# Second batch's attention in a fused attention and mixture-of-experts kernel: its place among the first group's matmuls

## The chip, the cores and the metric

The kernel runs on one core of one Trainium2 chip. The metric is the device time of one execution in microseconds (us), of which the median of several runs counts.

## What is computed

Three stages follow each other. In the reference, cut to what matters:

```
scores = q @ k.T / sqrt(64)             # 4 batches, 8 heads, 576 tokens, head width 64
scores += -2**-(h+1) * (i - j)          # kept where 0 <= i - j < 128, else -1e9
x = softmax(scores) @ v                 # as 2304 tokens x 512

g   = x @ w_gate                        # 512 -> 1536
x   = (g * sigmoid(g) * (x @ w_val)) @ w_out

# then 8 experts, the two best of each token by noisy logits:
out = sum over 2 of  weight * (relu(x @ w1[e]) @ w2[e])
```

## The kernel before

**Groups.** The 2304 tokens go through the gated layer in four groups of 512, 640, 512 and 640 tokens (`GRP`), one for each batch of attention. A group that begins before its batch takes 64 tokens of the batch ahead (`hold`). Attention of batch 0 runs first, alone. After that the work of group b and the attention of batch b+1 are interleaved.

**Precision.** A float32 number is held as a rounded high part and a low part (float32r, two slots of one tile), and a product is three matmuls (`three`, L295 to L297). Splitting takes a copy on ScalarE (ACT in the profile) and a subtraction on VectorE (DVE) or GpSimd (POOL).

**Weights.** During group 0 each of 36 weight blocks of 128x512 is read from memory in an unusual layout (`cs`), rebuilt by one pass on ACT (L227), one on POOL (L228) and two on DVE (L229, L230), written to a scratch tensor for later groups, and split by ACT (L270) and by POOL or DVE in turn (L271). `Convert.one` and `Stream.split` do this.

**A group** (`mlp1`) has two lists of quanta. `hidden` makes the 12 blocks of the hidden layer, two weight blocks each; in group 0 a quantum is half a weight block, six matmuls of 512 columns, so there are 48. Its results go through `sg`: tanh on ACT (L571), two passes on DVE that each read a PSUM bank (L572, L576), a copy on ACT that makes the high part `hT` (L577) and the subtraction that makes the low part (L578). `rows` is the second matmul, 24 quanta of six matmuls too, which read `hT`. So group 0 has 72 quanta.

**Attention** of a batch after the first (`attention`) is four pairs of heads, each a chain of 12 steps: transposes of q and k (L352, L356), evacuated by ACT (L361, L363); the scores of nine 64-row units in two sets, of five and four (`qk4`, L430), on the same two PSUM banks; for each set bias and minimum on DVE (L394), exp on ACT (L397), reciprocal on DVE (L398, L399) and normalization on POOL (L403); five transposes of the result (`pt`, L447), evacuated by ACT (L450, L452, L454, L463); and two products with v (`pv`, L477), whose result is copied by ACT (L493, the high part) and subtracted by DVE (L494, the low part) into `xT`, the input of the next group. Chunk c of the contraction of group b+1 reads what pair c wrote, so the last quarter of each of its accumulations needs the last pair.

**Order.** `merge(a, b, lead)` deals the steps of attention out over the quanta. That is the order in which the code is written. The instructions' order on each engine is made from it by the framework's scheduler, which moves ahead what it takes to be ready; on the chip each engine runs its own list in order. SyncE (SP) issues the loads and the stores of the scratch tensor in order too.

Of the kernel before, what the change touches and what calls it, by code (L numbers as in the profile page):

```python
# [22 lines left out]
def f32(ap):  # L23
    return ap.bitcast(F32)
# [3 lines left out]
def tile_alibi_window_attention__swiglu__noisy_top2_moe(  # L28
# [15 lines left out]
    nc = tc.nc  # L44
    B, H, S, D = q.shape
# [8 lines left out]
    HP = H // 2  # L54
# [22 lines left out]
    def bank(i):  # L77
        return psum.tile([128, 512], F32, name=f"b{i}", tag=f"b{i}")
# [36 lines left out]
    def load_nat(t, src, b, p, rest=None):  # L115

        eng = nc.scalar if src is k and (b, p) == (0, 0) else nc.sync
        for i in range(2):
            eng.dma_start(t[:, 0:4, i, :], src[b, 2 * p + i, 0:512, :].rearrange("(i p) d -> p i d", p=128))
        eng.dma_start(t[0:64, 4] if rest is None else rest, src[b, 2 * p:2 * p + 2, 512:576, :].rearrange("h p d -> p h d"))  # L120
        return t
# [46 lines left out]
    def buffers(b, p):  # L168
        return SET[p % 2 if b == 0 else 0]

    def load_qk(b, p):
        qn, kn = (buffers(b, p).nat(x) for x in ("qn", "kn"))
        NAT[b, p, "q"] = load_nat(qn, q, b, p)
        NAT[b, p, "k"] = load_nat(kn, k, b, p, qn[64:128, 4])

    def load_v(b, p):
        bf = buffers(b, p)
        NAT[b, p, "i"] = bf.nv % 2
        bf.nv += 1
        load_nat(bf.v[NAT[b, p, "i"]], v, b, p)  # L180
# [20 lines left out]
    class Convert:  # L201
# [7 lines left out]
        def load(self):  # L209
            m = self.n["l"]  # L210
            if m == UB:
                return
            self.n["l"] += 1
            t = cvp.tile([128, KC, 256], I32, name="cs", bufs=5)
            nc.sync.dma_start(t, dsrc[m])
            self.raw[m] = t.rearrange("p k (f w) -> p (k f) w", w=2)
# [76 lines left out]
    def three(ps, st, mv, first, last):  # L293

        nc.tensor.matmul(ps, st(0), mv(0), start=first, stop=False, skip_group_check=True)  # L295
        nc.tensor.matmul(ps, st(0), mv(1), start=False, stop=False, skip_group_check=True)  # L296
        nc.tensor.matmul(ps, st(1), mv(0), start=False, stop=last, skip_group_check=True)  # L297
# [4 lines left out]
    def new_xt(i, dt=F32R):  # L302
        return main.tile([128, 2, KC * GW], dt, name=f"xT{i % 2}")
# [4 lines left out]
    def xt_part(b, s):  # L308
        return XT[b][:, s, :].rearrange("p (c s) -> p c s", c=KC)

    def blocks(b):
        return GRP[b][1] // 128
# [21 lines left out]
    def attention(b, bk):  # L334
# [3 lines left out]
        def pair_items(p):  # L338
# [37 lines left out]
            def vp():  # L376
                st["v"], st["pt"] = bf.v[NAT[b, p, "i"]], bf.pt
                nxt(load_v)
# [118 lines left out]
            def nxt(load):  # L497
                n = p + (2 if b == 0 else 1)
                if n < HP:
                    load(b, n)  # L500
                elif b + 1 < B and n == HP:
                    load(b + 1, 0)

            def first():
# [8 lines left out]
                if (b, p) == (0, 1):  # L513
                    bias(p)

            rest = lambda: (tr("t")(), nxt(load_qk))
            v0 = lambda: (vp(), pt(0)())
            if b == 0:
# [17 lines left out]
    def gbank(b):  # L536
        gcount[0] += 1
        l = (0, 1, 2) if b < B - 1 else (0, 1, 2, 4, 5)
        return bank(l[gcount[0] % len(l)])

    def mlp1(b):

        base = b * UB
        n = GRP[b][1]
        cut = (0, n) if n <= 512 else (0, n // 2, n)

        def hh(s, f, sl):
            t, f = (HT[0], f) if f < NFA else (HT[1], f - NFA)
            return t[:, s, f * GW + sl.start:f * GW + sl.stop]

        def gv(f):
            st = {}

            def go(which, half, cs):
                def run():
                    u = base + 2 * f + which
                    sl = slice(cut[half], cut[half + 1])
                    w_ = sl.stop - sl.start
                    if cs.start == 0:
                        if half == 0:  # L560
                            ws.split(u + 3)
                        st["ps", which, half] = gbank(b)
                    w, ps = ws.tile[u], st["ps", which, half]
                    for c in range(cs.start, cs.stop):
                        three(ps[:, :w_], lambda s: w[:, s, c * 128:(c + 1) * 128],
                              lambda s: xt_part(b, s)[:, c, sl], c == 0, c == KC - 1)
                    if cs.stop < KC:
                        return
                    if which == 0:
                        t = wpool[1].tile([128, HW], F32, name="sg", bufs=3)[:, :w_]  # L570
                        nc.scalar.activation(t, ps[:, :w_], AF.Tanh, scale=0.5)  # L571
                        nc.vector.scalar_tensor_tensor(t, t, 1.0, ps[:, :w_], op0=OP.add, op1=OP.mult)  # L572
                        st["t", half] = t
                    else:
                        t = st["t", half]
                        nc.vector.scalar_tensor_tensor(t, t, 0.5, ps[:, :w_], op0=OP.mult, op1=OP.mult)  # L576
                        nc.scalar.activation(hh(0, f, sl), t, AF.Copy)  # L577
                        nc.vector.tensor_sub(hh(1, f, sl), t, f32(hh(0, f, sl)))  # L578
                return run
            parts = [slice(0, KC)] if len(cut) > 2 else [slice(0, 2), slice(2, KC)]  # L580
            return [go(w, h, cs) for w in range(2) for h in range(len(cut) - 1) for cs in parts]

        hidden = []
        for f in range(NF):
            hidden += gv(f)

        def yo(f, half):
            def run():
                u = base + 2 * NF + f
                if half == 0:  # L590
                    ws.split(u + 3)
                w = ws.tile[u]
                if f == 0 and half == 0:
                    std.l = dict(std.yo[blocks(b)])
                    YB1[b] = [bank(i) for i in range(blocks(b))]
                for i in range(2) if half == 0 else range(2, blocks(b)):
                    ps = YB1[b][i]
                    three(ps, lambda s: hh(s, f, slice(i * 128, (i + 1) * 128)), lambda s: w[:, s, :], f == 0, f == NF - 1)
                    if f == NF - 1:
                        if i == 0:  # L600
                            X2[b] = new_xt(b, F32)
                        o = X2[b][:, 0, i * DM:(i + 1) * DM]
                        if i % 2:
                            nc.vector.tensor_copy(o, ps)
                        else:
                            nc.scalar.activation(o, ps, AF.Copy)
                        r0 = GRP[b][0] + i * 128
                        nc.gpsimd.dma_start(x2d[r0:r0 + 128, 0:DM], o)
                if f == NF - 1 and half:
                    std.l = dict(std.gv)  # L610
            return run

        return hidden, [yo(f, h) for f in range(NF) for h in range(2)]
# [329 lines left out]
        scat[e, j] = s  # L943


    def merge(a, b, lead=0):
        n = 0
        for i, f in enumerate(a):
            f()
            while n < len(b) and (n + 1) * (len(a) - lead) <= (i + 1) * len(b):  # L950
                b[n]()
                n += 1
        for g in b[n:]:
            g()
# [22 lines left out]
    for b in range(B - 1):  # L977
        side = (post(b - 1, std) if b else []) + attention(b + 1, std)
        if b == 1:
            side.insert(len(side) // 2, zero_out)  # L980
        hidden, rows = mlp1(b)
        if b == 1:
            merge(hidden, side)
            merge(rows, [])
        else:
            merge(hidden + rows, side, 4)
        if b == 0:
            cv_cm.__exit__(None, None, None)
    b = B - 1
# [6 lines left out]
    side = post(b - 1, std) + route(0, T3, rt, True)  # L996
# [5 lines left out]
    n = len(side)  # L1002
# [3 lines left out]
    hidden, rows = mlp1(b)  # L1006
# [56 lines left out]
    with tc.If(n_over > 0):  # L1063
        with tc.tile_pool(name="ov", bufs=1) as ov:
            for e in range(E):
# [5 lines left out]
                with tc.For_i(CAP, n_e) as j:  # L1071
# [10 lines left out]
                    t = bank(0)  # L1082
# [49 lines left out]
```

## Time and profile before

| | |
|---|---|
| median of 3 runs | 1105.17 us (1104.94 to 1105.54) |
| profiled execution | 1102.93 us, its span 1101.1 us |
| TensorE (PE) busy | 1061.1 us, 96% |
| DVE, ACT, POOL busy | 525.6 us (48%), 477.7 us (43%), 444.6 us (40%) |
| mean granted TensorE clock | 0.995 |

PE's list begins with attention of batch 0; group 0's matmuls follow, mixed with attention of batch 1; from 191.93 us on they are those of group 1. A share of the whole span says little here, since the stages differ: in the first 150 us DVE is busier than anywhere else. Times below are us from the span's start; "busy" of PE is modelled, and the idle time before an instruction is what counts.

### The profile page before, as it was taken

How to read it: one execution, taken by the hardware profiler on the slowest of the kernel's cores; microseconds unless marked ns; L12 is line 12 of the kernel's file. 1: busy time of each engine (PE TensorE's matmuls, PEld its weight loads, DVE VectorE, ACT ScalarE, POOL GpSimd, SP SyncE). 2: the span in 40 equal slices, each digit the busy share in tenths (PEclk: the TensorE clock that was granted, in tenths of full speed). 3: DMA queues.
4: the chain of work that ended last, by engine and by line, in shares of the span. 5: the costliest groups of instructions: out<-in, count | busy, mean ns of one | idle time of the engine just before them, and what ended most of it. 6: DMA issues, size and time to landing. Idle time of an engine off the chain costs nothing. (4 is left out here: it accounts for less than half of the span.)

```text
span 1101.1 us, 18525 instructions
## 1 busy us (share of the span) xinstructions
PE 1061.1 (96%) x6694; PEld 905.7 (82%) x6694; DVE 525.6 (48%) x1258; ACT 477.7 (43%) x1229; POOL 444.6 (40%) x540
## 2 busy tenths in 40 slices
PE   6899999999999999999999999999999999999996
PEld 4566777989988777688997887988889898989894
DVE  7879973355410444124675345535353534343321
ACT  6666664466632466444543324424242323232210
POOL 5655654344434454443388323314141414141301
PEclk9999999999999999999999999999999999999998
DMA  8999754433323234331333506626263636353201
GB/s 205 260 290 300 249 178 117 123 91 85 88 73 117 82 101 105 87 109 58 87 90 115 179 5 198 196 87 201 87 188 93 184 93 187 103 168 111 71 28 42
DMA packets 158901, 143.93 MB, mean 131 GB/s; under 512 B 68238, under 2 KB 122542, under 8 KB 158800
## 3 DMA queue, kind: packets, MB, share of 16 engines
q1 hardware_dynamic: 147152, 108.89, 34.5%
q0 software_dynamic: 10448, 33.47, 9.4%
q8 instruction: 55, 0.90, 0.3%
q10 hardware_dynamic: 1200, 0.30, 0.1%
q14 instruction: 46, 0.38, 0.1%
HBM read 113.84 MB, written 28.91 MB: 130 GB/s over the span
## 5 line engine op out<-in xcount | busy, mean ns | idle before, releaser
L271 POOL TENSOR_TENSOR wu<-wst,wu 128x512 fp32r<-128x512 f32 x126 | 166.5, 1325 | 191.5 <-ACT wu L270 187.1
L270 ACT ACTIVATE wu<-wst 128x512 fp32r<-128x512 f32 x272 | 169.9, 629 | 137.1 <-PE b L297 63.0
L895 PE MATMUL b<-xT,wu 128*128 128x304 f32 (+2 forms) x1536 | 222.4, 303 | 1.2 <-ACT xT L882 0.6
L895 PEld LDWEIGHTS b<-xT,wu 128*128 128x128 f32 x1536 | 216.8, 188 | 5.0 <-DVE xT L883 1.9
L295 PE MATMUL b<-xT,wu 128*128 128x320 f32 (+1 forms) x576 | 200.4, 352 | 3.2 <-DVE sg L572 2.1
L296 PE MATMUL b<-xT,wu 128*128 128x320 f32 (+1 forms) x576 | 197.4, 343 | 0.8 <-DVE xT L494 0.6
L297 PE MATMUL b<-xT,wu 128*128 128x320 f32 (+1 forms) x576 | 197.0, 342 | 0.0
L295 PE MATMUL b<-wu,hTa 128*128 128x512 f32 (+1 forms) x482 | 192.8, 401 | 1.0 <-DVE sg L576 1.0
L296 PE MATMUL b<-wu,hTa 128*128 128x512 f32 (+1 forms) x482 | 188.9, 392 | 0.0
L297 PE MATMUL b<-wu,hTa 128*128 128x512 f32 (+1 forms) x482 | 187.5, 393 | 0.0
L271 DVE TENSOR_TENSOR wu<-wst,wu 128x512 fp32r<-128x512 f32 x146 | 105.8, 729 | 47.1 <-ACT wu L270 44.7
L295 PEld LDWEIGHTS b<-xT,wu 128*128 128x128 f32 x576 | 108.2, 189 | 17.8 <-issue 4.0
L296 PEld LDWEIGHTS b<-xT,wu 128*128 128x128 f32 x576 | 108.8, 189 | 10.1 <-issue 1.7
L297 PEld LDWEIGHTS b<-xT,wu 128*128 128x128 f32 x576 | 108.6, 189 | 9.0 <-issue 1.6
L902 DVE SCALAR_TENSOR_TENSOR hTa<-b,hTa 128x304 fp32r<-128x304 f32 (+2 forms) x128 | 57.2, 471 | 118.0 <-ACT hTa L901 117.9
L872 POOL DMA_INDIRECT xo<-x2d,gib x37 | 36.8, 994 | 183.4 <-PE b L879 165.5
L901 ACT ACTIVATE hTa<-b 128x304 fp32r<-128x304 f32 (+2 forms) x128 | 50.2, 423 | 139.3 <-PE b L895 139.1
L295 PEld LDWEIGHTS b<-wu,hTa 128*128 128x128 f32 (+1 forms) x482 | 88.9, 185 | 21.3 <-issue 1.8
L297 PEld LDWEIGHTS b<-wu,hTa 128*128 128x128 f32 (+1 forms) x482 | 88.7, 184 | 20.6 <-issue 0.2
L296 PEld LDWEIGHTS b<-wu,hTa 128*128 128x128 f32 (+1 forms) x482 | 89.1, 185 | 18.4 <-issue 0.2
L403 POOL TENSOR_SCALAR sx<-sx,sm 128x192 f32<-128x192 f32 (+2 forms) x126 | 60.2, 494 | 65.3 <-DVE sm L399 45.3
L882 ACT ACTIVATE xT<-b 128x512 fp32r<-128x512 f32 (+1 forms) x40 | 22.7, 572 | 136.4 <-PE b L879 136.4
(196 smaller groups left out, 1314.6 us busy)
## 6 DMA issues: line engine op xcount, KB each, us to landing
wst<-in_moe_w_dram SPq DMA_DIRECT2D x128, 256.0 KB, 3.2
wst<-wscr SPq DMA_DIRECT2D x108, 256.0 KB, 2.7
wscr<-wst SPq DMA_DIRECT2D x36, 256.0 KB, 3.6
cs<-in_moe_w_gate_dram SPq DMA_DIRECT2D x12, 512.0 KB, 6.2
cs<-in_moe_w_val_dram SPq DMA_DIRECT2D x12, 512.0 KB, 5.6
cs<-in_moe_w_out_dram SPq DMA_DIRECT2D x12, 512.0 KB, 4.6
out_dram<-zero SPq DMA_DIRECT2D x1, 4608.0 KB, 20.2
x2d<-xT POOLq DMA_DIRECT2D x18, 256.0 KB, 4.0
```

The lines of the kernel that those rows point to most:

```text
L270: nc.scalar.activation(t[:, 0, :], s, AF.Copy)
L271: self.eng(n).tensor_sub(t[:, 1, :], s, f32(t[:, 0, :]))
L295: nc.tensor.matmul(ps, st(0), mv(0), start=first, stop=False, skip_group_check=True)
L296: nc.tensor.matmul(ps, st(0), mv(1), start=False, stop=False, skip_group_check=True)
L297: nc.tensor.matmul(ps, st(1), mv(0), start=False, stop=last, skip_group_check=True)
L403: nc.gpsimd.tensor_scalar(x, x, sm[:, i:i + 1], 1.0, op0=OP.mult, op1=OP.mult)
L872: nc.gpsimd.indirect_dma_start(out=x[0:r], out_offset=None, in_=x2d[0:GRP[-1][0], :] if (e, g) == (0, False) else x2d, in_offset=bass.Indi ...
L882: nc.scalar.activation(d[0], tv, AF.Copy)
L895: nc.tensor.matmul(ps[g][:, 0:hi - lo], w[:, a, c * 128:(c + 1) * 128], xgt(e, m, g)[:, c, 0:hi - lo], start=(c == 0 and a + m == 0), stop ...
L901: nc.scalar.activation(d, ps[g][:, 0:hi - lo], AF.Relu)
L902: nc.vector.scalar_tensor_tensor(h2[1][:, f, lo:hi], ps[g][:, 0:hi - lo], 0.0, f32(d), op0=OP.max, op1=OP.subtract)
```

## The change

Attention of batch 1 is dealt out over quanta 22 to 68 of group 0's 72, where it was dealt out over quanta 0 to 68. `merge` gets an argument `late` for this. The loads of its first pair are no longer asked for by attention of batch 0, but by an entry put in at place 12 of `hidden`. And in group 0 the subtraction that makes the low part of `hT` (L578) goes to POOL.

```diff
-                elif b + 1 < B and n == HP:
+                elif 0 < b < B - 1 and n == HP:
                     load(b + 1, 0)
...
-                        nc.vector.tensor_sub(hh(1, f, sl), t, f32(hh(0, f, sl)))
+                        (nc.vector if b else nc.gpsimd).tensor_sub(hh(1, f, sl), t, f32(hh(0, f, sl)))
...
-    def merge(a, b, lead=0):
+    def merge(a, b, lead=0, late=0):
...
-            while n < len(b) and (n + 1) * (len(a) - lead) <= (i + 1) * len(b):
+            while n < len(b) and (n + 1) * (len(a) - lead - late) <= (i + 1 - late) * len(b):
...
-            merge(hidden + rows, side, 4)
+            if b == 0:
+                hidden.insert(12, lambda: (load_qk(1, 0), load_v(1, 0)))
+            merge(hidden + rows, side, 4, 0 if b else 22)
```

What the scheduler makes of it differs from pair to pair. Counted in quanta of six matmuls on PE's list, the first score matmuls of the four pairs stand at quantum 4, 22, 40 and 60 before, and at quantum 4, 37, 54 and 76 after. Quantum 72 is the first of group 1. From quantum 82 on the lists of PE are the same.

The first place is PE around that seam. Before, the last pair's scores were done eleven quanta ahead; its transposes (`sx`) and the first product with v stand among the last matmuls of group 0 (`hTb`), and the row with `xT1` and 320 columns opens group 1:

```order
L447 MATMUL b6_2114<-ident_74,sx4_96 128x128
L447 MATMUL b6_2114<-ident_74,sx4_96 64x128
L477 MATMUL b7_2125<-pt_91,v1_90 64x128 x4
L297 MATMUL b2_1827<-wu_2158,hTb_735 128x512
L295 MATMUL b3_1828<-wu_2158,hTb_735 128x512
L296 MATMUL b3_1828<-wu_2158,hTb_735 128x512
L297 MATMUL b3_1828<-wu_2158,hTb_735 128x512
L295 MATMUL b0_2295<-xT1_801,wu_2214 128x320
```

After, the last pair's scores (L430) themselves stand in group 1, with three matmuls of group 1 between them and the transposes that need their softmax:

```order
L430 MATMUL b5_2059<-kT_1881,qT_97 64x192 x2
L295 MATMUL b2_2268<-xT1_1071,wu_2197 128x320
L296 MATMUL b2_2268<-xT1_1071,wu_2197 128x320
L297 MATMUL b2_2268<-xT1_1071,wu_2197 128x320
L447 MATMUL b6_2102<-ident_74,sx0_92 64x128
L447 MATMUL b6_2102<-ident_74,sx0_92 128x128
L447 MATMUL b6_2113<-ident_74,sx1_93 128x128 x3
L477 MATMUL b7_2142<-pt_91,v1_90 64x128 x2
L447 MATMUL b6_2131<-ident_74,sx4_96 128x128
L447 MATMUL b6_2131<-ident_74,sx4_96 64x128
L477 MATMUL b7_2142<-pt_91,v1_90 64x128 x4
L447 MATMUL b6_2162<-ident_74,sx2_94 128x128 x3
```

So a whole chain of a pair moved from among group 0's matmuls to behind the seam. The two rows that follow the last of these are the first matmuls that read the last pair's chunk.

The second place is DVE in the same pair: the end of the first set (its minimum `mn`, then the reciprocal of its sums `sm`) and the start of the second. Before:

```order
L394 ISA mn_1961 128x1
L398 TENSOR_SCALAR sm_1962<-sm_1962 128x5
L399 RECIPROCAL sm_1962<-sm_1962 128x5
L271 TENSOR_TENSOR wu_2158<-wst_2102,wu_2158 128x512
L494 TENSOR_TENSOR xT1_801<-b7_1995,xT1_801 128x320
L394 ISA sx2_94,mn_2041<-b4_2031,tab0_76 128x192
```

After, the first set's sums are `sm_2004`, the second set's `sm_2069` (its minimum `mn_2068`):

```order
L394 ISA mn_2068 128x1
L399 RECIPROCAL sm_2004<-sm_2004 128x5
L398 TENSOR_SCALAR sm_2069<-sm_2069 128x4
L399 RECIPROCAL sm_2069<-sm_2069 128x4
L494 TENSOR_TENSOR xT1_1071<-b7_2142,xT1_1071 128x256
```

The reciprocal of the first set moved behind the whole second set's L394, which in turn stands behind the L494 of the pair before.

The third place is POOL in the hidden part of group 0. After:

```order
L271 TENSOR_TENSOR wu_1333<-wst_1255,wu_1333 128x512
L578 TENSOR_TENSOR hTa_723<-sg_1181,hTa_723 128x512
L228 TENSOR_SCALAR cs_1135<-cs_1135 128x512
L228 TENSOR_SCALAR cs_1219<-cs_1219 128x512
L271 TENSOR_TENSOR wu_1444<-wst_1336,wu_1444 128x512
L578 TENSOR_TENSOR hTa_723<-sg_1281,hTa_723 128x512
```

Where L228 and L271 of the weights stood alone, one L578 stands between them for every two weight blocks, twelve in all.

## Rows read from the trace of the kernel before

**Rows 1.** Three stretches: length, busy us and instructions by engine, clock, DMA share, GB/s.

```profile
62.33:155.10 92.77, 84.86 (x509) 64.25 (x505) 83.77 (x170) 64.84 (x174) 58.03 (x67) 0.98 0.84 264
101.60:107.60 6.00, 3.85 (x24) 2.78 (x24) 5.96 (x19) 4.29 (x14) 2.06 (x2) 0.73 0.90 269
155.10:205.24 50.14, 50.01 (x323) 40.95 (x323) 18.23 (x46) 24.82 (x68) 19.86 (x25) 1.00 0.43 124
```

**Rows 2.** PE's waits from 62 to 205 us: total us, times, longest.

```profile
PE b L295 <- DVE sg L572: 2.1, 2, 1.7
PE b L295 <- DVE sg L576: 1.9, 2, 1.0
PE b L477 <- ACT pt L463: 0.8, 1, 0.8
```

**Rows 3.** PE in order of time around 104 us: start, us, instruction, idle before.

```profile
103.78 1.09 PE L430 MATMUL b<-kT,qT 64*64 64x192 f32 x16 [2.15 <-DVE mn L394]
...
105.40 0.63 PE L296 MATMUL b<-xT,wu 128*128 128x512 f32 x1
105.83 0.63 PE L297 MATMUL b<-xT,wu 128*128 128x512 f32 x1
```

**Rows 4.** Groups by line and form, 62 to 205 us: busy us, mean ns; idle before.

```profile
L271 POOL TENSOR_TENSOR wu<-wst,wu 128x512 fp32r<-128x512 f32 x20 | 27.9, 1393 | 23.9 <-ACT wu L270 22.5 <-DMA qn<-in_q_dram 1.3
L229 DVE SCALAR_TENSOR_TENSOR wst<-wst,cs 128x512 int32<-128x512 int32 x30 | 26.2, 877 | 11.1 <-POOL cs L228 11.1
L230 DVE SCALAR_TENSOR_TENSOR wst<-cs,wst 128x512 int32<-128x512 int32 x30 | 25.9, 870 | 0.1
...
L572 DVE SCALAR_TENSOR_TENSOR sg<-sg,b 128x512 f32<-128x512 f32 x12 | 8.1, 674 | 0.7 <-ACT sg L571 0.7
L578 DVE TENSOR_TENSOR hTa<-sg,hTa 128x512 fp32r<-128x512 f32 x9 | 7.2, 799 | 1.0 <-ACT hTa L577 0.9
...
L578 DVE TENSOR_TENSOR hTb<-sg,hTb 128x512 fp32r<-128x512 f32 x3 | 2.1, 690 | 0.7 <-ACT hTb L577 0.7
```

**Rows 5.** POOL and DVE side by side near 94 us, in order of time.

```profile
93.89 1.23 POOL L228 TENSOR_SCALAR cs<-cs 128x512 f32<-128x512 f32 x1 [1.04 <-issue]
94.52 1.13 DVE L229 SCALAR_TENSOR_TENSOR wst<-wst,cs 128x512 int32<-128x512 int32 x1
```

**Rows 6.** Batch 1's second pair, first set: scores, first DVE row, normalization on POOL.

```profile
95.30 0.88 PE L430 MATMUL b<-kT,qT 64*64 64x192 f32 x20
...
101.77 0.34 DVE L394 CUSTOM_DVE_ANT_0 sx<-b,tab 128x192 f32<-128x192 f32 x1
...
106.94 2.19 POOL L403 TENSOR_SCALAR sx<-sx,sm 128x192 f32<-128x192 f32 x5 [0.36 <-DVE sm L399]
```

**Rows 7.** The same of batch 1's last pair: scores, last DVE row, normalization.

```profile
171.25 0.88 PE L430 MATMUL b<-kT,qT 64*64 64x192 f32 x20
...
173.38 0.08 DVE L394 DVE_READ_ACCUMULATOR2_ANT mn<- 128x1 f32 x1
...
175.34 2.37 POOL L403 TENSOR_SCALAR sx<-sx,sm 128x192 f32<-128x192 f32 x5 [3.01 <-ACT wu L270]
```

**Rows 8.** ACT evacuating one set of transposes, in order of time.

```profile
171.36 0.39 ACT L454 ACTIVATE pt<-b 128x256 f32<-128x256 f32 x1 [0.38 <-PE b L447]
171.64 0.54 ACT L463 ACTIVATE pt<-b 64x128 f32<-64x128 f32 x2
```

**Rows 9.** PE at the start of group 1, in order of time.

```profile
191.93 0.31 PE L295 MATMUL b<-xT,wu 128*128 128x320 f32 x1
192.07 0.31 PE L296 MATMUL b<-xT,wu 128*128 128x320 f32 x1
...
197.52 0.49 PE L447 MATMUL b<-ident,sx 128*128 128x128 f32 x3
197.94 0.66 PE L477 MATMUL b<-pt,v 128*64 128x128 f32 x8
198.53 0.41 PE L295 MATMUL b<-xT,wu 128*128 128x320 f32 x1
...
205.24 0.42 PE L677 MATMUL b<-xT,wgn 128*32 128x128 f32 x6
```

## The prediction

> **What bounds the kernel now.** I read first the table of stretches, then PE's waits, then PE in order of time around the longest wait, and last the groups by line. PE is busy 96% of the span, so only stretches where it is not can give anything, and of these the change touches one: group 0, from 62 us on. There the stretches [rows 1] show 7.9 us of PE idle to 155 us (92.77 less 84.86) and 0.1 us after that (50.14 less 50.01). DVE is busy 83.8 of 92.8 us in the first part and 5.96 of 6.00 us around the longest wait, but only 18.2 of 50.1 us in the second [rows 1]. So PE waits for DVE, which is full early and has room late. The waits say the same: two for L572 and two for L576, which free the PSUM banks of the hidden layer, 4.0 us in all [rows 2], and 2.15 us before a set of scores, for the minimum of the set before it, which holds its banks [rows 3]. Behind that idle time the granted clock is low: 0.73 on average over 6.00 us [rows 1], which is 3.2 us at the level of 1.2 GHz, and the matmuls follow each other at 0.43 us there [rows 3]. Half of 3.2 us is lost, 1.6 us. All that PE loses in this part of the program is thus 8.0 + 1.6 = **9.6 us**, and no better place for attention can win more.
>
> **What the change moves, and what it can't move.** The matmuls, their number and their columns stay. Work that goes from one place on PE to another costs nothing by itself. From quantum 82 on PE's list is unchanged, so everything is decided before the row that now starts at 205.24 us [rows 9].
>
> **The gain in group 0.** The first pair stays where it was, at quantum 4. The two longest waits for L572 and L576, 1.7 and 1.0 us [rows 2], lie at 67 and 71 us, ahead of quantum 12, where PE's list is the same: 2.7 us stay. At most 9.6 - 2.7 = 6.9 us can go. What relieves DVE: twelve subtractions leave it, 7.2 + 2.1 = 9.3 us [rows 4], and three of four pairs come later. What loads it: without attention PE asks for the weights faster. For two weight blocks DVE needs two passes L229 and L230 each, 2 x (0.877 + 0.870) = 3.5 us, one L271 of some 0.7 us (as L572, the nearest row that POOL does not disturb), and L572 with L576, 1.35 us [rows 4]: 5.5 us. PE needs for them 24 matmuls of 512 columns at 0.23 us (half of the 0.43 at half clock [rows 3], and a little): 5.5 us. The two are level, so DVE stays close behind PE and doesn't get ahead. Before, the second pair's scores on PE were 6.5 us ahead of DVE's first row for them (95.30 to 101.77) [rows 6]. Of what stands ahead of that place now and did not before, DVE has 8 weight blocks (14.0 us), 3 L271 (2.1) and 7 of L572 and L576 (4.7), less 5 L578 (4.0) [rows 4]: 16.8 us, up to 19 with what POOL adds (below). PE has 88 matmuls and four products, 88 x 0.228 + 0.6 = 20.6 us. So DVE is still 3 to 5 us behind. The normalized rows of that set then come about 2 us after PE wants its transposes (0.8 us of matmuls stand between). I put new waits at 3.7 us in all: these 2, half a microsecond for the third pair, and 1.2 us of the small ones as in the row for L463 [rows 2]. Gain 6.9 - 3.7 = **3.2 us**. Bounds: 6.9 us if nothing new waits, and -2 us if the second pair waits as long as before, the clock falls again (2.15 + 1.6 us) and the new waits come on top.
>
> **The subtraction on GpSimd.** L271 is the same operation on the same shape there: 12 x 1.39 = 16.7 us [rows 4], against 58 of 92.8 us that POOL is busy [rows 1]. Its readers are the `rows` quanta from 48 on, so nobody waits for its result. Queued behind it on POOL are L228 and L271 of the weights; no wait of PE there is for a weight (the long ones are for `sg` and the scores [rows 2, 3]), so I cost that at nothing. If that cover is gone, each costs up to 1.4 us.
>
> A price of it is on DVE. A DVE pass with two operands in SBUF is slowed when POOL works: L229 takes 1.13 us beside an L228 [rows 5], and the means of L229 and L230 are 0.88 and 0.87 us, while L572, with one operand in PSUM, stays at 0.67 [rows 4]. That is 0.2 us x 60 = 12 us over POOL's 58 us or more, 0.2 us of DVE for each us of POOL: 16.7 us of subtractions give back 3 of the 9.3 us.
>
> The Trainium skill (SBUF — State Buffer, Who interferes with whom) says that a DVE instruction with two SBUF inputs contends with a GpSimd instruction that reads SBUF, and that the later one fully blocks until the first is done. It speaks against this edit: by it a DVE pass that meets a subtraction waits for what is left of 1.39 us, and if each meets one halfway DVE loses 12 x 0.7 = 8.4 us, nearly all of the 9.3. The rows agree in kind (0.67 against 0.88) and give the smaller price.
>
> **The loads.** The nine DMAs of the first pair stand on SP within a few places of where they stood, among the same weight loads. Nothing, and a few tenths either way.
>
> **The loss at the seam.** Now the last pair's chain stands behind group 0's last matmul, with few matmuls around it, and the last quarter of every accumulation of group 1 needs it. I add it up from the seam, with PE's list in hand. (1) To the scores: 24 matmuls of 320 columns at 0.145 us (191.93 to 192.07) 3.5 us, three groups of transposes at 0.42 (197.52 to 197.94) 1.3 us [rows 9]; they share one bank, and two of its evacuations, 0.9 us each [rows 8], are waited for: 6.6 us. (2) Scores and minimum, 171.25 to 173.46: 2.2 us [rows 7], 8.8. (3) The second set's L394 now stands behind the L494 of the pair before, and that behind an evacuation and a product: 1.3 us, then four units at the pace of (2), 1.8 us, and only then the first set's reciprocal: 11.9. (4) Normalization starts 0.4 us later and takes 2.4 us for five [rows 7]: 14.7. (5) Transposes and evacuation 1.3 us, then the next transposes, the product and its copy at about that again, 1.4 us: **17.4 us** from the seam to the first matmul of the last chunk. PE's own work in that time: 27 matmuls 3.9, 29 transposes at 0.14 us 4.1, 18 products at 0.59 for four [rows 9] 2.7, 18 score matmuls at 0.88 for ten [rows 7] 1.6: 12.3 us. So 5.1 us are lost, and I add 1 us for the second product, whose chain is mostly covered by 18 matmuls. Before, the same stretch loses 0.1 us [rows 1]. The idle times inside are of the length of the one in [rows 3], so the clock should fall here; much of it falls on idle time: 0.6 us of the 1.6. Loss **6.7 us**. Bounds: from scores to normalization I have 5.7 us; the quiet pair took 4.1 (171.25 to 175.34) [rows 7], and without the clock and half of the last 1 us that is 4 us in all; the pair in the full stretch took 11.6 (95.30 to 106.94) [rows 6], which makes 12.6 us. I stay near the quiet one, since DVE and ACT are only half busy there [rows 1].
>
> **Sum.** 6.7 - 3.2 = +3.5 us. The profiled execution took 1102.93 us and would take 1106.4. The median is 2.24 us above it, so I predict **1108.7 us**. Ends: 4 - 6.9 = -2.9 and 12.6 + 2 = +14.6 us.
>
> **Rivals.** *Faster:* DVE gets free in the hidden part, all 6.9 us return, and the seam goes at the quiet pair's pace, 4 us: -2.9 us, 1102.3. For it speaks that DVE's relief is largest just where PE waits; against it that DVE and PE need the same 5.5 us for two blocks. It decides from where DVE reaches the second pair's L394 no more than 2 us after its scores and the seam loses under 4.7 us. *No change:* the waits only move, 5 lost at the seam and 5 won: 1105.2. For it speaks that both sums are of one size. *Slower by more:* the GpSimd subtractions block DVE and hold up the weights' passes queued behind them, so that the gain is nothing: +6.7 us, 1111.9. For it speaks [rows 5], against it the mean of 0.2 us for each us of POOL. The rule cited above is this rival's, and would give this time if every subtraction met a pass. That the change doesn't do what it says is true in part, since the first pair stays; it is in the sum.
>
> **How the numbers follow.** Forecast 0.50, faster 0.15, no change 0.20, slower by more 0.15. A measurement of this kernel tells 0.2%, 2.2 us, from no change. The forecast's own spread leaves 0.07 of its 0.50 within that. So faster 0.15, same 0.27, slower 0.58. The range from 1103 to 1114.5 leaves out the last of the faster case and the upper end of the seam.
>
> **What would show it.** In the new profile: group 1's first matmul starts 8 to 11 us earlier than 191.93, since 6.5 us of the last pair's work stand behind it now; the row at 205.24 starts 2 to 6 us later; PE's waits there name L403, L463 or L493, some 5 to 8 us in all; the 2.15 us wait is gone or smaller; L578 shows twelve times on POOL at 1.3 to 1.5 us. The forecast is wrong if PE idles under 4 us between the seam and that row, or if the waits ahead of the seam fall under 3 us.

## The result, and the profile after

The changed kernel takes **1119.65 us** (median of 4 runs, 1118.53 to 1121.32) against 1105.36 us of the kernel before in the same comparison: ratio 1.0122, 95% interval 1.0095 to 1.0149. That is about 13.5 us slower. The forecast was slower, 1108.7 us, with a range that ended at 1114.5: the direction is right, the time lies outside.

The profiled execution took 1118.53 us, its span is 1116.7 us, 15.6 us more than before. PE's busy share is the same (96%) and its mean clock close (0.991), so again only stretches tell something. The first fence answers [rows 1]; columns as there. Its second row is group 0 from 62.33 us to group 1's first matmul (191.45 us), the third goes from there to the L677 row:

```profile
62.33:155.10 92.77, 80.14 (x422) 60.45 (x419) 82.81 (x137) 57.59 (x140) 67.79 (x69) 0.98 0.81 256
62.33:191.45 129.12, 116.49 (x640) 88.96 (x637) 97.69 (x174) 76.13 (x193) 87.07 (x91) 0.99 0.69 217
191.45:218.88 27.43, 23.44 (x194) 18.69 (x192) 7.64 (x31) 13.59 (x49) 6.07 (x13) 0.88 0.38 102
```

The reader is to see three things. PE idles 12.6 us ahead of the seam (129.12 less 116.49) where it idled 7.9 [rows 1]. DVE, which lost eleven of the twelve subtractions and one of three pairs of attention from the first of these stretches, is nearly as busy as before: 82.8 against 83.8 us. And behind the seam PE idles 4.0 us (27.43 less 23.44) and runs at a clock of 0.88, which is some 3 us more.

PE's waits from 62 to 230 us (total us, times, longest), beside [rows 2]:

```profile
PE b L295 <- DVE sg L572: 4.8, 4, 1.4
PE b L447 <- POOL sx L403: 4.8, 3, 2.2
PE b L447 <- ACT pt L463: 1.9, 3, 0.7
PE b L430 <- DVE mn L394: 1.5, 2, 1.3
PE b L295 <- DVE sg L576: 1.2, 1, 1.2
```

The wait for L572 grew from 2.1 to 4.8 us, and the wait for the normalized rows (L403) from 0.5 to 4.8. In the kernel before it was this:

```profile
PE b L447 <- POOL sx L403: 0.5, 1, 0.5
```

Behind the seam the last pair's chain looks so (PE and POOL in order of time: start, us, instruction, idle before), to be read beside [rows 9]:

```profile
191.45 0.39 PE L295 MATMUL b<-xT,wu 128*128 128x320 f32 x1
...
198.26 0.88 PE L430 MATMUL b<-kT,qT 64*64 64x192 f32 x20
...
203.57 3.45 POOL L403 TENSOR_SCALAR sx<-sx,sm 128x192 f32<-128x192 f32 x9 [9.49 <-ACT sx L397]
...
204.34 0.67 PE L447 MATMUL b<-ident,sx 128*64 128x128 f32 x2 [1.71 <-POOL sx L403]
...
205.57 0.52 PE L447 MATMUL b<-ident,sx 128*128 128x128 f32 x3 [0.57 <-ACT pt L463]
...
207.01 0.69 PE L447 MATMUL b<-ident,sx 128*128 128x128 f32 x2 [0.55 <-ACT pt L463]
...
209.23 0.90 PE L295 MATMUL b<-xT,wu 128*128 128x320 f32 x2
...
218.88 0.42 PE L677 MATMUL b<-xT,wgn 128*32 128x128 f32 x6
```

Last, the groups that answer [rows 4], from 62.33 to 205.24 us (busy us, mean ns, idle before):

```profile
L229 DVE SCALAR_TENSOR_TENSOR wst<-wst,cs 128x512 int32<-128x512 int32 x29 | 30.8, 1066 | 8.3 <-POOL cs L228 8.3
L230 DVE SCALAR_TENSOR_TENSOR wst<-cs,wst 128x512 int32<-128x512 int32 x30 | 28.9, 970 | 0.3
L271 DVE TENSOR_TENSOR wu<-wst,wu 128x512 fp32r<-128x512 f32 x16 | 14.9, 928 | 3.4 <-ACT wu L270 3.1
L578 POOL TENSOR_TENSOR hTa<-sg,hTa 128x512 fp32r<-128x512 f32 x9 | 13.3, 1480 | 5.2 <-ACT hTa L577 5.2
L572 DVE SCALAR_TENSOR_TENSOR sg<-sg,b 128x512 f32<-128x512 f32 x12 | 8.1, 676 | 1.8 <-ACT sg L571 1.8
```

L229 went from 877 to 1066 ns, L230 from 870 to 970; L572, with an operand in PSUM, stayed at 0.68 us.

**Where the 15.6 us are.** What the lower clock costs is added up here over slices of 2 us, in both kernels alike: busy time times the missing share of the clock. Ahead of the seam: 12.6 us idle and 1.7 by the clock, 14.3, against 7.9 + 1.7 = 9.6 before: 4.7 more. From the seam to the L677 row: 4.0 + 3.2 = 7.2 us against 0.1 [rows 1]: 7.1 more. The L677 row itself is 13.64 us later (218.88 less 205.24), so 1.8 us are neither idle time nor clock by these views. From 62.33 us to that row both kernels have the same 831 matmuls, so these 1.8 us must lie inside rows that count as busy: a matmul that nothing follows counts 0.3 to 0.4 us, where in a row the same one costs 0.15 [rows 9]. No run prices that by itself. Further on, one more fall of the clock, which the forecast had no term for, costs 1.4 us (15.90 us busy at 0.91) behind a wait of 1.92 us. The same wait was 1.61 us before, and the clock stayed. The second row is of the kernel before:

```profile
468.00:486.00 18.00, 15.90 (x85) 11.71 (x78) 2.75 (x14) 9.59 (x29) 11.70 (x16) 0.91 0.37 98
...
454.40:471.00 16.60, 14.77 (x86) 10.76 (x79) 2.76 (x14) 9.52 (x29) 11.80 (x16) 1.00 0.37 106
```

### The profile page after: what moved, and what is told of

Its sections match the earlier page's. It is cut to its first block, busy times and chain, and to the rows that moved or that the text cites. A ratio compares the mean times of both kernels' runs of the same rounds, so it can differ in the third digit from the quotient of the medians.

```text
span 1116.7 us, 18534 instructions
## 1 busy us (share of the span) xinstructions
PE 1067.3 (96%) x6694; PEld 909.0 (81%) x6694; DVE 528.7 (47%) x1246; ACT 478.8 (43%) x1229; POOL 457.3 (41%) x552
## 4 chain that ended last, share of the span: by engine, by line
PE 83%; DVE 6%; ACT 4%; DMA 3%; issue 2%; POOL 1%; ACTq 0%; SPq 0%; POOLq 0%; DVEq 0%
PE b L295 19%; PE b L297 18%; PE b L296 18%; PE b L895 18%; PE b L477 3%; PE b L447 2%; PE b L879 1%; PE b L430 1%; DVE wst L229 1%; ACT sx L397 1%; PE b L352 1%; DVE wst L230 1%; DMA xo<-x2d,gib 1%; DMA wst<-in_moe_w_dram 1%; PE b L664 1%
## 5 line engine op out<-in xcount | busy, mean ns | idle before, releaser
L271 POOL TENSOR_TENSOR wu<-wst,wu 128x512 fp32r<-128x512 f32 x126 | 165.2, 1314 | 188.6 <-ACT wu L270 186.9
L270 ACT ACTIVATE wu<-wst 128x512 fp32r<-128x512 f32 x272 | 169.9, 630 | 148.3 <-PE b L297 57.8
L271 DVE TENSOR_TENSOR wu<-wst,wu 128x512 fp32r<-128x512 f32 x146 | 108.9, 750 | 47.4 <-ACT wu L270 45.2
L403 POOL TENSOR_SCALAR sx<-sx,sm 128x192 f32<-128x192 f32 (+2 forms) x126 | 59.2, 486 | 77.1 <-DVE sm L399 30.4
```

The source lines that it names most:

```text
L270: nc.scalar.activation(t[:, 0, :], s, AF.Copy)
L271: self.eng(n).tensor_sub(t[:, 1, :], s, f32(t[:, 0, :]))
L403: nc.gpsimd.tensor_scalar(x, x, sm[:, i:i + 1], 1.0, op0=OP.mult, op1=OP.mult)
```

## Experiments: the engine of the subtraction

Ratios below are to the kernel before, measured on the same chip, with 95% intervals. All kernels are ordered anew by the scheduler, so the places of the scores shift by some quanta from run to run; where that matters it is said.

**The changed kernel with L578 back on VectorE.**

```diff
-                        (nc.vector if b else nc.gpsimd).tensor_sub(hh(1, f, sl), t, f32(hh(0, f, sl)))
+                        nc.vector.tensor_sub(hh(1, f, sl), t, f32(hh(0, f, sl)))
```

> The changed kernel with group 0's L578 back on VectorE; the late placing and the early loads stay. Theory A (the subtraction on GpSimd slows VectorE's two-operand passes by as much as it takes off VectorE: L229, L230 and L271 there took 11.2 us more in the changed kernel, L578 took 9.3 us less): VectorE has about 2 us less to do before group 1, POOL 17 us less, group 1's first matmul comes 2 to 4 us earlier, time 1115 to 1118. Theory B (only the place of attention counts, not the engine of L578): 1118.5 to 1121. Theory C (the forecast's own step: GpSimd takes 9.3 us off and costs 3): group 0 gets 4 to 6 us worse, 1123 to 1126.

Measured 1114.31 us, 1.0065 (1.0048 to 1.0081): 0.57% less than the changed kernel. To give VectorE the work back made the kernel faster, a little more than A expected; theories B and C fall. PE idles 8.7 us ahead of the seam instead of 12.6, although DVE's sum is no smaller: L229, L230, L271 and L578 take 77.1 us there, the first three 74.6 in the changed kernel.

**The kernel before with only L578 moved** (its line as in the changed kernel).

> The kernel before with only group 0's L578 moved to GpSimd; attention and loads as before. Theory A (lock as dear as the relief): VectorE's busy time up to 206 us within 3 us of before, time 1105 to 1108, no gain. Theory B: 1104.5 to 1106. Theory C (relief of 6 us net): the waits for L572, L576 and for the scores' minimum go, 1100 to 1103.

Measured 1111.43 us, 1.0034 (1.0017 to 1.0050): slower than A's range, against C. PE idles 12.7 us in group 0 instead of 7.9. DVE's passes show why (62.33 to 205.24 us):

```profile
L229 DVE SCALAR_TENSOR_TENSOR wst<-wst,cs 128x512 int32<-128x512 int32 x30 | 33.1, 1112 | 11.3 <-POOL cs L228 11.3
L230 DVE SCALAR_TENSOR_TENSOR wst<-cs,wst 128x512 int32<-128x512 int32 x30 | 26.4, 889 | 0.3
L271 DVE TENSOR_TENSOR wu<-wst,wu 128x512 fp32r<-128x512 f32 x16 | 13.7, 857 | 4.0 <-ACT wu L270 4.0
```

Together 73.2 us. Before, the same three groups and L578 took 72.7 us in this stretch (25.5 + 25.9 + 12.0 + 9.3, with one L229 less). VectorE got nothing. The row of the kernel before that [rows 4] does not have is

```profile
L271 DVE TENSOR_TENSOR wu<-wst,wu 128x512 fp32r<-128x512 f32 x16 | 12.0, 747 | 3.3 <-ACT wu L270 3.0
```

**L578 on neither of the two**, in the changed kernel and in the kernel before:

```diff
-                        nc.vector.tensor_sub(hh(1, f, sl), t, f32(hh(0, f, sl)))
+                        if b:
+                            nc.vector.tensor_sub(hh(1, f, sl), t, f32(hh(0, f, sl)))
+                        else:
+                            nc.scalar.activation(hh(1, f, sl), t, AF.Copy, scale=0.0)
```

> The changed kernel with group 0's L578 replaced by a copy on ScalarE that writes zeros (the low part of the hidden layer is left out of the second matmul in group 0), so neither VectorE nor GpSimd has it. The order of the scores on PE is that of the changed kernel. Theory A (lock): L229 and L230 return to means of about 0.88 us, the waits for L572 and L576 before the second pair mostly go, time 1111 to 1115. Theory B (the place alone): 1118.5 to 1121. The part behind the seam should not change in either: 27 us from group 1's first matmul to the L677 row.

> The kernel before with group 0's L578 replaced by a copy on ScalarE that writes zeros (the low part of the hidden layer is left out of the second matmul in group 0). This is what the forecast took GpSimd's subtraction to be: VectorE's relief without its price. Theory A (VectorE's 9.3 us are worth something to PE when GpSimd does not take them): PE's idle time from 62 us to group 1 falls from 7.9 to 3 to 5 us, time 1099 to 1103. Theory B (VectorE's load there does not decide): 1104.5 to 1107.

Measured, in the changed kernel: 1108.06 us, 1.0014 (1.0001 to 1.0028), even less than A expected; in the kernel before: 1102.08 us, 0.9953 (0.9934 to 0.9972). So the work taken off VectorE is worth 0.5% if GpSimd doesn't get it. PE's idle time fell less than A had it in the kernel before, from 7.9 to 6.7 us and not to 3 to 5; the clock did not fall from 62 us to group 1. The two stretches of the changed kernel with this edit, ahead of the seam and behind it, and DVE's passes:

```profile
62.33:182.00 119.67, 114.91 (x655) 88.78 (x655) 89.95 (x175) 81.98 (x206) 66.91 (x79) 1.00 0.75 237
182.00:209.00 27.00, 23.31 (x197) 18.49 (x197) 7.73 (x31) 13.83 (x49) 6.18 (x13) 0.87 0.37 103
```

```profile
L229 DVE SCALAR_TENSOR_TENSOR wst<-wst,cs 128x512 int32<-128x512 int32 x30 | 28.3, 946 | 8.8 <-POOL cs L228 7.7 <-DMA wst<-wscr 0.5 <-DMA kn<-in_k_dram 0.5
L230 DVE SCALAR_TENSOR_TENSOR wst<-cs,wst 128x512 int32<-128x512 int32 x30 | 24.0, 800 | 0.5
L271 DVE TENSOR_TENSOR wu<-wst,wu 128x512 fp32r<-128x512 f32 x16 | 14.3, 894 | 1.5 <-ACT wu L270 1.4
```

PE idles 4.8 us ahead of the seam at full clock, and the stretch behind the seam is as in the changed kernel (3.7 us idle, clock 0.87). The three groups are 66.6 us against 74.6 in the changed kernel: twelve subtractions on GpSimd cost VectorE 8.0 us, if anything more, since the stretch of the changed kernel has one L229 less. In the order of the kernel before it is 73.2 less 64.8 (25.2 + 25.6 + 14.0), 8.4 us.

## Experiments: the seam and the place

**Ending eight quanta earlier**, with L578 on GpSimd, on ScalarE (zeros) and on VectorE:

```diff
-            merge(hidden + rows, side, 4, 0 if b else 22)
+            merge(hidden + rows, side, 4 if b else 12, 0 if b else 22)
```

> The changed kernel with attention dealt out over quanta 22 to 60 instead of 22 to 68; the last pair's scores then stand at quantum 65 and 67, no chain behind the seam. Theory S (the seam alone costs 6.8 us of idle time and half clock): that is gone, 2 us come back as waits among the rows of group 0, time 1112 to 1116. Theory D (what is taken from the seam is lost again in the denser part): 1118 to 1121. Group 0's hidden part should lose as much PE time as in the changed kernel, 12 us of idle time between 62 us and the last pair.

> The changed kernel with both suspects gone: attention dealt out over quanta 22 to 60, so that no chain stands behind the seam, and group 0's L578 replaced by the copy of zeros on ScalarE (its low part left out). If seam and GpSimd's subtraction are the two causes and add up (0.88% and 1.08% of the time by the runs so far, from 1.22% above before): 0.7% under before, 1097 to 1101. If the one hides the other: 1102 to 1106. Against the kernel before with the same copy on ScalarE it tells what the late place is worth by itself: the forecast had it worth some us, a rival nothing.

> The changed kernel with attention dealt out over quanta 22 to 60 and L578 on VectorE as before: only the late place and the early loads are left, with no chain behind the seam. If the parts add (0.57% for the subtraction, 0.88% for the seam): 0.2% under before, 1103 to 1106. If the late place costs by itself (three pairs in 30 quanta, VectorE full from 80 to 140 us): 1107 to 1111.

Measured: 1111.14 us, 1.0034 (1.0021 to 1.0046) with GpSimd; 1103.99 us, 0.9971 (0.9957 to 0.9985) with ScalarE; 1111.60 us, 1.0043 (1.0025 to 1.0062) with VectorE. In the first, the stretch from group 1's first matmul to the L677 row:

```profile
198.41:212.82 14.41, 14.17 (x116) 12.69 (x114) 3.55 (x8) 5.62 (x19) 3.38 (x5) 1.00 0.45 131
```

There the seam costs 0.24 us at full clock where it cost 7.2, and the whole is 0.88% less than the changed kernel: theory S, a little beyond it. Ahead of the seam PE idles 11.7 us, the 12 that were expected. The parts do not add, though. With seam and GpSimd's subtraction both gone, 0.7% under before was expected and 0.29% came; the kernel before with the same copy on ScalarE is at 0.9953, no worse. **The late place by itself is worth nothing** (together with its early loads, which no run parts from it). And with VectorE doing the subtraction, ending earlier brought 0.22% only, which is not clear of noise: there a new wait stands among the rows of group 0, 2.75 us for L403, and the clock is 0.83 from 160 to 180 us. At this place GpSimd's subtraction shows no price in time (1.0034 against 1.0043), though DVE's three groups take 76.7 us with it and 66.5 without it, where L578 adds 11.8. The two orders differ in that wait, which the GpSimd kernel has not; whether the wait hides the price is not shown.

```profile
164.42 0.82 PE L447 MATMUL b<-ident,sx 128*64 128x128 f32 x2 [2.75 <-POOL sx L403]
```

**The same with an earlier start**, quanta 12 to 60 (`0 if b else 12`), L578 on VectorE.

> As the kernel above, but attention dealt out over quanta 12 to 60: second pair's scores at quantum 28 instead of 37, so that less is packed into the last 36 quanta. If density is what costs in the late place: 1 to 3 us less than the kernel above, 1102 to 1105. If the hidden part's VectorE is the bound whatever the place: the same as the kernel above, within 1 us.

Measured 1107.40 us, 1.0001 (0.9989 to 1.0014): 0.42% less than from quantum 22 on. That is a larger step than the 1 to 3 us of the density theory, and a time above its range. It fits that density costs: early and even is as good as before, late is not.

## Experiments: GpSimd's reads, or its queue

**A memset in place of the subtraction**, in the kernel before:

```diff
+                            nc.gpsimd.memset(f32(hh(1, f, sl)), 0.0)
```

> The kernel before with group 0's L578 replaced by a GpSimd memset of zeros of the same tile (the low part of the hidden layer is left out of the second matmul in group 0): GpSimd has an instruction at the same place of its queue that reads nothing. Theory L (what costs is that GpSimd's subtraction reads two operands from SBUF beside VectorE's passes): L229 and L230 stay at 0.83 to 0.88 us, time as with the copy on ScalarE, 1100 to 1104. Theory Q (what costs is one more instruction in GpSimd's queue ahead of the weights' L228 and L271): between that and the subtraction on GpSimd, 1105 to 1109.

Measured 1101.94 us, 0.9970 (0.9957 to 0.9983). It doesn't tell the two apart: with nothing to wait for, the memsets were put at 47.6 to 59.3 us, ahead of the work in question.

So three memsets of the tile that L578 read were put behind these, which have to wait for ScalarE's L577 as L578 did:

```diff
+                            for _ in range(3):
+                                nc.gpsimd.memset(t, 0.0)
```

> The changed kernel with L578 of group 0 replaced by three GpSimd memsets of the tile that L578 read, which wait for ScalarE's L577 as L578 did: 12 x 3 x 0.53 = 19 us in GpSimd's queue against 17.6, writes without reads (the low part of the hidden layer is left out of the second matmul in group 0: zeros, written early). Theory L (reads beside VectorE's passes): VectorE's L229, L230 and L271 fall from 74.6 us to 65 to 68 us in all, time as with the copy on ScalarE, 1105 to 1110. Theory Q (queue): 74 us or less, but PE waits on as in the changed kernel, 1115 to 1120.

> The same replacement in the kernel before. Theory L: 1100 to 1104, as with the copy on ScalarE. Theory Q: 1108 to 1112, as with the subtraction on GpSimd.

The memsets stand where the subtraction stood (in the changed kernel: count, shortest, median and longest duration in ns, first and last start):

```profile
L583 POOL MEMSET sg<- x36: 519/526/543, 75.4 to 148.6; 128x512 f32 x36
```

Measured, in the kernel before: 1101.26 us, 0.9950 (0.9934 to 0.9966), the same as with the copy on ScalarE, although GpSimd is busy 91.8 us from 62.33 to 205.24, nearly as long as with the subtraction (93.6). DVE's passes take 64.8 us:

```profile
L229 DVE SCALAR_TENSOR_TENSOR wst<-wst,cs 128x512 int32<-128x512 int32 x30 | 29.6, 989 | 10.9 <-POOL cs L228 10.8
L230 DVE SCALAR_TENSOR_TENSOR wst<-cs,wst 128x512 int32<-128x512 int32 x30 | 23.2, 776 | 0.6
L271 DVE TENSOR_TENSOR wu<-wst,wu 128x512 fp32r<-128x512 f32 x16 | 12.0, 752 | 0.5 <-ACT wu L270 0.3
```

In the changed kernel: 1111.07 us, 1.0035 (1.0020 to 1.0049), just above the range of theory L and well under that of Q; DVE's passes take 64.0 us against 74.6, and PE idles 4.2 us ahead of the seam, though at a clock of 0.97. So it is mainly the reads, and the queue is at most a small part. What that part is, 0.2% in the changed kernel's order (against the copy on ScalarE) and nothing in the order before, stays open.

## Experiments: the same exchange in the other direction

**The weights' subtraction L271**, same operation and shape, shared between GpSimd and VectorE before. All on GpSimd, two of three on VectorE, all on VectorE, in the kernel before; the last:

```diff
-    ws = Stream([wscr[u] for u in range(UB)] * B, place1, lambda n: nc.vector if n < UB and n % 2 else nc.gpsimd, conv)
+    ws = Stream([wscr[u] for u in range(UB)] * B, place1, lambda n: nc.vector if n < UB else nc.gpsimd, conv)
```

> The kernel before with all weight subtractions L271 of group 0's stretch on GpSimd: the change's exchange once more, with 16 instead of 12 instructions, 12.0 us off VectorE and 22 us more on GpSimd. Theory L: VectorE's busy time stays within 4 us of before, GpSimd is full, time 1107 to 1114. Theory C: VectorE gets 12.0 less 4.4 us, 1100 to 1104.

> The kernel before with two of three weight subtractions L271 on VectorE, instead of one of two. Theory L: half way to the run with all of them there, 1102 to 1105. Theory C: 1106 to 1109.

> The kernel before with the 20 weight subtractions L271 that GpSimd has in group 0's stretch moved to VectorE too: the change's exchange in the other direction, same operation, same shape. Theory L (on GpSimd each takes from VectorE about what it takes off): VectorE's busy time up to 206 us stays within 4 us of before, GpSimd has 28 us less, time 1099 to 1104. Theory C (the forecast's rate, 0.2 us of VectorE for each us of GpSimd): VectorE has 13.6 less 5.6, that is 8 us more, and PE waits for it, 1109 to 1114.

Measured: all on GpSimd 1112.99 us, 1.0051 (1.0035 to 1.0067); two thirds on VectorE 1103.86 us, 0.9996 (0.9977 to 1.0015), no difference that can be told; all on VectorE **1100.06 us, 0.9944 (0.9926 to 0.9962)**, faster than both kernels. Theory C falls at both ends. With all on GpSimd, L229, L230 and L578 alone take 76.6 us on DVE, more than the 72.7 that they took together with L271 before. With all on VectorE its other passes shorten and PE's wait for L572 is 1.5 us, once:

```profile
L271 DVE TENSOR_TENSOR wu<-wst,wu 128x512 fp32r<-128x512 f32 x31 | 23.4, 759 | 5.8 <-ACT wu L270 5.8
L229 DVE SCALAR_TENSOR_TENSOR wst<-wst,cs 128x512 int32<-128x512 int32 x29 | 22.7, 795 | 4.2 <-POOL cs L228 4.2
L230 DVE SCALAR_TENSOR_TENSOR wst<-cs,wst 128x512 int32<-128x512 int32 x29 | 20.9, 726 | 0.0
...
L578 DVE TENSOR_TENSOR hTa<-sg,hTa 128x512 fp32r<-128x512 f32 x9 | 6.1, 675 | 0.0
```

Fifteen more L271 put 11.4 us on VectorE, and L229, L230 and L578 gave 9.0 back (51.7 us against 60.7). VectorE's sum is 2.4 us higher than before, yet PE idles 3.4 us instead of 7.9: the sum alone doesn't explain the gain; the long single passes and 18 us less on GpSimd have their part in it, which these runs don't separate.

The same edit in the changed kernel, and with attention over quanta 12 to 60 and L578 on VectorE:

> The changed kernel with the weights' subtractions L271 of group 0's stretch all on VectorE, L578 still on GpSimd: GpSimd has 28 us less, VectorE 20 passes of 0.68 us more. Theory L (what GpSimd takes from VectorE is what counts): GpSimd's L271 cost VectorE about what they took off, so VectorE's load is the same and GpSimd's queue is short, 1110 to 1115. Theory C (VectorE's own load counts): 8 us more VectorE work in a stretch where it is full, 1122 to 1128.

> Attention dealt out over quanta 12 to 60, L578 on VectorE, and the weights' subtractions L271 of group 0's stretch all on VectorE too: no two-operand subtraction is left on GpSimd there. If the two add (0.0% and -0.56%): 1099 to 1102, as the kernel before with the second edit alone. If density costs more now that VectorE has more of its own: 1102 to 1106.

Measured 1113.78 us, 1.0072 (1.0048 to 1.0095), and 1100.96 us, 0.9951 (0.9936 to 0.9967). Both as theory L had it; more work on VectorE made the changed kernel faster, and no placing that was tried beat the old one with all L271 on VectorE.

## Why the direction was right and the time wrong

**What bounds the kernel: right, though DVE's sum is not all of it.** With 8 us less on DVE, in the order before, the idle time fell from 7.9 to 6.7 us and the clock stayed at 1.00 up to 155 us. With all L271 on DVE its sum was higher, and the idle time fell to 3.4 us.

**The subtraction on GpSimd: this is the step that failed.** The forecast took its price on VectorE as 0.2 us for each us of GpSimd, the mean over all of GpSimd's work, and so 3 of the 9.3 us. (That mean mixes two stretches: its 60 passes lie between 62 and 205 us, its 58 us of GpSimd end at 155.) Measured, the price is 8.0 and 8.4 us (10.6 against the memsets), so hardly anything of the relief was left. The mean was the wrong price for what is added to it: twelve more instructions of 1.47 us, among passes that stand one behind the other on DVE, cost 0.45 us for each us (8.0 of 17.6), more than twice the mean.

Why the added ones cost more can be counted in the two traces, from 62.33 to 205.24 us, over the DVE passes L229, L230, L271 and L578 of 128x512, which take 0.68 us when nothing holds them up. Every pass that took over 0.1 us longer ended 0.52 to 0.56 us after an instruction of POOL had ended. Before, these were 22 of 87 passes, 13.2 us too long in all: ten behind the 20 L271 on POOL (9.1 us), nine behind the 29 L228 (3.8), three behind the 36 L403 (0.4). In the changed kernel they were 33 of 75 passes and 23.3 us, and eleven of the twelve L578 held one up, by 1.04 us each. So L228 and L403 had kept the mean low. The like row, L271, cost 0.46 us for each instruction, which would have made 5.5 us for twelve (an estimate), and L578 met a pass nearly every time where L271 did every second time.

What one meeting costs could be read from [rows 5], 1.13 us for a pass of 0.68, and in the changed kernel it is this (DVE, POOL and PE in order of time):

```profile
94.55 1.49 POOL L578 TENSOR_TENSOR hTa<-sg,hTa 128x512 fp32r<-128x512 f32 x1 [0.20 <-ACT hTa L577]
94.80 1.78 DVE L271 TENSOR_TENSOR wu<-wst,wu 128x512 fp32r<-128x512 f32 x1
...
96.00 1.09 POOL L228 TENSOR_SCALAR cs<-cs 128x512 f32<-128x512 f32 x1
96.51 1.12 DVE L230 SCALAR_TENSOR_TENSOR wst<-cs,wst 128x512 int32<-128x512 int32 x1
...
98.87 0.68 DVE L572 SCALAR_TENSOR_TENSOR sg<-sg,b 128x512 f32<-128x512 f32 x1
...
99.61 0.50 PE L295 MATMUL b<-xT,wu 128*128 128x512 f32 x1 [1.32 <-DVE sg L572]
```

L271 starts 0.25 us after L578, takes 1.78 us instead of 0.68 and ends 0.54 us after L578 does; L230 meets the next instruction of GpSimd; both stand ahead of L572 on DVE's list, for which PE then waits 1.32 us. The Trainium skill (SBUF — State Buffer, Who interferes with whom) says that a VectorE instruction with two SBUF inputs contends with a GpSimd instruction that reads SBUF, over a shared pair of ports that is an exclusive lock, and that the order of issue decides which of the two blocks. The trace agrees: in the two meetings shown and in [rows 5] the DVE pass ends 0.53 or 0.54 us after the POOL instruction, a little less than its own 0.68. The estimate of 8.4 us that the prediction worked out from that rule, and set aside for 3, has the size that was measured. That it fits so closely is partly luck: it let each subtraction hold up a pass by 0.7 us, where eleven did so by 1.04, and in exchange L271 on POOL held up passes by 6.8 us instead of the 10.0 with the copy on ScalarE. The same section of the Trainium skill says that a GpSimd instruction that only writes SBUF does not contend in this way; the 36 memsets agree (64.8 us of passes with them, 64.8 with the copy on ScalarE, in the kernel before).

**The gain in group 0: wrong in size and sign.** Forecast -3.2 us, measured +4.7. DVE reached the second pair's first row 7.4 us behind its scores, where 3 to 5 us were forecast. PE then waited three times, and the clock fell (PE, DVE and POOL in order of time; then a stretch as in [rows 1]):

```profile
123.05 0.88 PE L430 MATMUL b<-kT,qT 64*64 64x192 f32 x20
...
130.48 0.34 DVE L394 CUSTOM_DVE_ANT_0 sx<-b,tab 128x192 f32<-128x192 f32 x1
131.89 0.88 PE L430 MATMUL b<-kT,qT 64*64 64x192 f32 x16 [1.33 <-DVE mn L394]
134.72 3.27 POOL L403 TENSOR_SCALAR sx<-sx,sm 128x192 f32<-128x192 f32 x5 [0.35 <-DVE sm L399]
135.87 0.30 PE L447 MATMUL b<-ident,sx 128*64 128x128 f32 x1 [2.21 <-POOL sx L403]
137.24 0.33 PE L447 MATMUL b<-ident,sx 128*128 128x128 f32 x1 [0.84 <-POOL sx L403]
...
138.00:142.00 4.00, 4.00 (x13) 3.09 (x13) 2.80 (x8) 3.47 (x14) 4.00 (x4) 0.57 0.66 247
```

That is the case of the lower bound: the second pair waited again, 4.4 us in all, and the clock fell again. (The bound was put at -2 us; its own terms, 3.2 less 2.15 and 1.6, make -0.6.) With the subtraction on neither engine the same placing lost 4.8 us ahead of the seam against 9.6 before, a gain of 4.8, inside the bounds given. But the relief alone, without moving attention, brought as much in the end (0.9953 against 0.9971 for the late place without its seam). "DVE and PE are level at 5.5 us" held for a DVE without the price: by the measured means two weight blocks cost DVE 5.7 us there and 6.4 in the changed kernel.

The price makes the exchange even on DVE, and so explains that nothing was gained. It doesn't by itself explain a loss: DVE's sum is about the same with L578 on GpSimd as on DVE (74.6 against 77.1 us with the late place, 73.2 against 72.7 without), yet PE idles 12.6 us against 8.7, and 12.7 against 7.9. What differs is where the long passes stand, ahead of L572 in the rows near 95 us, and that GpSimd's own work took longer too: the five L403 above took 3.27 us, those of the last pair before 2.37 [rows 7]. How much each of these makes was not separated.

**GpSimd's queue at nothing: held, for the most part.** PE waits 0.6 us for weights ahead of the seam (0.4 for L270, 0.2 for L271), and the memsets in the queue of the kernel before cost nothing.

**The seam: the chain right, its loss right in part by luck.** 17.4 us were added up from the seam to the first matmul of the last chunk; it starts at 209.23, 17.8 us behind 191.45. Loss forecast 6.7 us, measured 7.2. But the forecast had 6.1 us of idle time and 0.6 by the clock, and it was 4.0 and 3.2: two errors that nearly cancel. The waits are mostly for L403 and L463, as said. Ending earlier took them away. The 1.8 us that are neither idle nor clock were not in the sum.

**The signs to look for.** L578 stands twelve times on POOL at 1.47 us on average, and the 2.15 us wait became 1.33: right. Group 1's first matmul came 0.48 us earlier, not 8 to 11, and the L677 row 13.64 us later, not 2 to 6: both mostly because group 0 lost time instead of gaining it, and because PE's work behind the seam grew by 5.2 us (121.69 us busy ahead of it before, 116.49 after), not 6.5. The waits behind the seam, 4.0 us in all, stayed under the 5 to 8 of the sign, and at 3.99 us (27.43 less 23.44) the idle time there even met, by 0.01 us, the sign under which the forecast called itself wrong. The rival "slower by more" had the mechanism, at 1111.9 us: it let the gain be nothing, where it became a loss of 4.7. Had the subtraction cost neither engine anything, the time would have been inside the forecast's range: that kernel measured 1108.06 us, 0.14% above the kernel before, some 1.5 us where 3.5 were forecast.

## What to carry to other kernels

Before a two-operand pass is moved from VectorE to GpSimd, count the passes with two SBUF operands that it will meet and price one meeting by a row of the same kind; don't spread a mean over all of GpSimd's work. Here a pass ended half a microsecond after the GpSimd instruction that it met, and eleven of twelve met one. The move gave back nearly all that it took, and moving the same kind of pass the other way was the better change. A chain that is dealt out later must still end ahead of the work that needs it: add it up in program order from the seam, as was done here, and compare with a run that ends earlier.

## What the runs showed of the hardware

GpSimd's own instruction is not of one length: with L578 moved in the kernel before, the same shape took 1.28 us at the shortest and 1.75 at the longest. A GpSimd memset of 128x512 took 0.53 us, and in neither kernel with the memsets does a longer DVE pass end just behind one. The five L403 of one set took 2.19 us at one place [rows 6] and 3.27 at another. The granted clock fell to 0.54 on average from 206 to 212 us behind idle times of 1.71, 0.57 and 0.55 us, and to 0.91 over 18 us behind a single one of 1.92 us, while behind 1.61 us, at the same place of the program, it stayed at 1.00.
